# A linear-attention layer with a squared-ReLU network: r loaded for four batches at once, the diagonal added at y's eviction, the state moved to GpSimd

## The chip, the cores and the metric

One Trainium2 chip, one core. Each engine (TensorE = PE, VectorE = DVE, ScalarE = ACT, GpSimd = POOL, SyncE = SP) works through its own instructions in the order in which the program lists them. The metric is device time in microseconds: median 190.98 of three runs (190.21 to 191.86).

## What is computed

```python
# B 4, H 8, S 768, D 48; d_model = H*D = 384, d_ff 2048
for t in range(S):
    cur = einsum('bhd,bhe->bhde', u * kt, vt)
    y[:, :, t] = einsum('bhd,bhde->bhe', rt, state + cur)
    state = w[:, :, None] * state + einsum('bhd,bhe->bhde', kt, vt)
x = y.transpose(0, 2, 1, 3).reshape(B * S, H * D)
h = relu(x @ w_in)
out = (h * h) @ w_out
```

Inputs and output are float32; the kernel multiplies in bfloat16.

## The kernel before

The sequence is cut into 6 chunks of 128 tokens; a unit is one chunk of one batch, so there are 24 units, the four batches of chunk 0 first. In a unit the recurrence is a product of matrices: r scaled by powers of w (`wpos`) and k by inverse powers (`wneg`) are multiplied to a 128x128 table per head (`at`), the part above the diagonal is kept (`mask`), and the table times v, plus r times the state of the chunks before (`stb`), plus the diagonal with u, is y.

**Loads.** `load` (L190 to L197) brings r, k and v of one unit, one SP transfer each, with 128 tokens on 128 partitions; each head and token is a piece of 48 numbers, 192 bytes. Six units' loads fit at a time. The network's weights come in four quarters each, I0 to I3 for `w_in` and O0 to O3 for `w_out`, issued from POOL by `weights` (L199 to L208); a copy of one column of a k tile (`gate`) makes POOL wait for that k first.

**A unit's steps.** DVE scales r and k into one padded bf16 tile, 64 columns a head (L217). ACT casts v to `vb` (L221). The scaled tile is turned so that the head's columns lie on partitions: for the first six units (NPE) by eight PE transposes into PSUM (L236) and one ACT copy (L241), later by one transposing transfer on SP (L226). DVE multiplies turned r and k (`rk`, L246); PE makes `at` with eight products (L254), and from `rk` and u the diagonal's weight per token and head (`diag`, L268); DVE masks (L262) and multiplies that weight with v (`dv`, L276). The state's product is eight PE products of 64 by 48, one a head (L285); DVE adds it to the float32 state (L295) and multiplies by the chunk's decay (L299; L293 does the first chunk's), and ACT casts it to `stb` in two halves (L305). The last chunk has no state step. y is summed in one PSUM tile: eight products with the masked table (L313), four with the state (L319), and one that adds `dv` by way of the identity (L324). ACT evicts y (L332), it is turned again, by three PE transposes and an ACT copy in the first six units (L343, L348), by a transposing transfer afterwards (L337).

**The network.** A unit's x goes through four quarters: 12 PE products (`mm1`, L358), Relu on ACT into float32 (L366), the square on DVE into bf16 (L370), and four PE products that sum in PSUM (`mm2`, L377). ACT copies the sum out (L384), and SP stores it (L388). Three PSUM banks are shared by h and the PE transposes, two by `at` and the state's product, two by o; y has one.

**The order of the work.** It is not written by hand: the class `Plan` holds every step with its engine, a cost in microseconds, a rank, the steps that it needs and the buffers that it takes. `run` goes forward in time, and whenever an engine is free, takes of its steps that can start the one of lowest rank; the program is emitted in that order. All transfers count as one more engine, DMA, though the weights are issued from POOL. A step's rank grows by 4 a unit; `mm1` is put L1 = 10 ranks behind its unit, `mm2` L2 = 18. The front of the loads is a list: U0, U1, I0, U2, I1, U3, I2, I3, U4, O0 to O3, U5 (U is a unit's r, k and v). `room` has the buffers of each kind.

Of the kernel before, what the change touches and what calls it, by code (L numbers as in the profile page):

```python
# [79 lines left out]
def kernel(  # L80
# [11 lines left out]
    nc = tc.nc  # L92
# [10 lines left out]
    NPAD = 4  # L103

    const = ctx.enter_context(tc.tile_pool(name="const", bufs=1))
    loads = ctx.enter_context(tc.tile_pool(name="loads", bufs=6))
    work = ctx.enter_context(tc.tile_pool(name="work", bufs=4))
# [36 lines left out]
    iota_i = const.tile([128, 1], mybir.dt.int32)  # L144
    nc.gpsimd.iota(iota_i, pattern=[[0, 1]], base=0, channel_multiplier=1)
    up = const.tile([128, 1], F32)
    nc.vector.tensor_scalar(up, iota_i, 1.0, -float(C // 2), ALU.mult, ALU.add)
    down = const.tile([128, 1], F32)
    nc.vector.tensor_scalar(down, iota_i, -1.0, float(C // 2 - 1), ALU.mult, ALU.add)
    lnw = const.tile([128, dm], F32)  # L150
    nc.scalar.activation(lnw, w_bc, AF.Ln)
    wpos = const.tile([128, H, D], F32)
    nc.scalar.activation(wpos.rearrange("p h d -> p (h d)"), lnw, AF.Exp, scale=up)
    wneg = const.tile([128, H, D], F32)
    nc.scalar.activation(wneg.rearrange("p h d -> p (h d)"), lnw, AF.Exp, scale=down)

    rkw_b = [const.tile([128, 2, HP, 2, 64], BF16, name=f"rkw{n}") for n in range(NPAD)]
    for n in range(NPAD):
        for x in range(2):
            nc.vector.memset(rkw_b[n][:, x, :, :, D:], 0.0)  # L160
# [28 lines left out]

    def load(i, name):  # L190
        c, b = units[i]
        src = {"rt": r, "kt": k, "vt": v}[name]
        x = loads.tile([C, H, D], F32, name=name)
        nc.sync.dma_start(  # L194
            out=x, in_=src[b, :, c * C : (c + 1) * C, :].rearrange("h s d -> s h d")
        )
        tiles[i][name] = x  # L197
# [15 lines left out]
    def scale(i, x):  # L213
        t = tiles[i]
        t["rkw"] = rkw_b[i % NPAD]
        src, wx = (t["kt"], wneg) if x else (t["rt"], wpos)
        nc.vector.tensor_tensor(t["rkw"][:, x, :, :, :D], pair(src), pair(wx), ALU.mult)  # L217

    def cast_v(i):
        tiles[i]["vb"] = work.tile([C, H, D], BF16, name="vb")  # L220
        nc.scalar.copy(tiles[i]["vb"], tiles[i]["vt"])  # L221

    def turn_dma(i):
        t = tiles[i]
        t["rkT"] = work.tile([128, 2, HP, C], BF16, name="rkT")
        nc.sync.dma_start_transpose(  # L226
            out=t["rkT"].rearrange("p a h c -> p (a h) c"),
            in_=t["rkw"].rearrange("p a h o e -> p (a h o e)"),
        )

    def turn(i, x):
        t = tiles[i]
        if x == 0:
            t["tp"] = ps_h.tile([128, 2, HP, C], BF16, name="h")
        for p in range(HP):
            nc.tensor.transpose(t["tp"][:, x, p, :], t["rkw"][:, x, p].rearrange("p o e -> p (o e)"), identb)  # L236

    def evict_rk(i):
        t = tiles[i]
        t["rkT"] = work.tile([128, 2, HP, C], BF16, name="rkT")  # L240
        nc.scalar.copy(t["rkT"], t["tp"])  # L241

    def rk(i):
        t = tiles[i]
        t["rk"] = work.tile([128, HP, C], BF16, name="rk")
        nc.vector.tensor_tensor(t["rk"], t["rkT"][:, 0], t["rkT"][:, 1], ALU.mult)  # L246

    def at(i):
        t = tiles[i]
        t["at"] = [ps_at.tile([C, HP, C], F32, name="at") for o in range(2)]  # L250
        for p in range(HP):
            for o in range(2):
                sl = slice(o * 64, o * 64 + 64)
                nc.tensor.matmul(  # L254
                    out=t["at"][o][:, p, :], lhsT=t["rkT"][sl, 1, p, :], rhs=t["rkT"][sl, 0, p, :],
# [17 lines left out]
    def diag_v(i):  # L273
        t = tiles[i]
        t["dv"] = work.tile([C, H, D], BF16, name="dv")
# [4 lines left out]
    def state_mm(i):  # L280
        t = tiles[i]
        t["s"] = ps_at.tile([128, HP, D], F32, name="at")
        for h in range(H):
            p, o = divmod(h, 2)
            nc.tensor.matmul(  # L285
                out=t["s"][o * 64 : o * 64 + 64, p, :], lhsT=t["rkw"][:, 1, p, o, :],
                rhs=t["vb"][:, h, :], start=True, stop=True,
            )

    def state_add(i):  # L290
        c, b = units[i]
        if c == 0:
            nc.vector.tensor_tensor(st32[b], tiles[i]["s"], wend, ALU.mult)  # L293
# [234 lines left out]
```

## Time and profile before

| | |
|---|---|
| median of three runs | 190.98 us |
| the profiled execution | 190.88 us, of which the span of its instructions 189.1 |
| busy in the span | PE 169.1, DVE 145.1, ACT 112.4, POOL 11.4 us |
| transfers on SP's queue | 104832 packets, 25.37 MB, 73.4% of 16 transfer engines' span |
| weights on POOL's queue | 3712 packets, 10.5% |
| one r, k or v load | 192 KB, from issue to landing 4.1, 3.9 and 4.4 us |
| granted PE clock | 0.996 |

Busy times are of instructions as the profiler records them; those of one engine can overlap by some tens of nanoseconds, and an engine's own sums over its groups are then larger than its busy time. Matmul ends are modelled, so starts are the surer times. A row of the timeline has the start, the length, the engine, the line, the operation, the tiles written and read, and the shapes; a row of the windows the stretch, its length, the busy time of PE, PE's weight loads, DVE, ACT and POOL (with the number of instructions), then the granted clock, the share of the transfer engines and GB/s.

### The profile page before, as it was taken

To read this page: it belongs to the slowest core of one execution; us is meant where nothing else is said; L and a number is where in the kernel's file an instruction comes from. 1 tells how busy PE (TensorE), PEld (TensorE's weight loads), DVE (VectorE), ACT (ScalarE), POOL (GpSimd) and SP (SyncE) were. 2 spreads that over 40 slices of the span, in tenths; PEclk is the share of its full clock that TensorE was granted. 3 is DMA by queue.
4 is the path that set the end of the run, shared out by engine and by line. 5 is a ranking of instruction groups with operands and counts; after the bars stand their busy time and mean duration, and the time that the engine had idled before them with its cause. 6 is when DMAs were issued, how large, how long until landed. Compare 5 with 4: busy or idle time off the path is not lost.

```text
span 189.1 us, 5640 instructions
## 1 busy us (share of the span) xinstructions
PE 169.1 (89%) x2346; PEld 131.0 (69%) x2346; DVE 145.1 (77%) x292; ACT 112.4 (59%) x224; POOL 11.4 (6%) x36
## 2 busy tenths in 40 slices
PE   0269889999999998899999999979999999999991
PEld 0147779677787866677767876758777787787860
DVE  3367679967999859798989998789998888845510
ACT  3537588767756757466467557645747555555511
POOL 2261370000000000000000000000000000000000
PEclk9999999999999999999999999999999999999998
DMA  5999999918997978787989779998998999210112
GB/s 104 179 182 217 212 211 194 190 25 207 159 224 155 123 166 192 147 179 168 172 181 203 145 144 214 100 203 171 190 192 170 183 179 168 68 32 30 45 42 85
DMA packets 109545, 29.07 MB, mean 154 GB/s; under 512 B 102736, under 2 KB 109520, under 8 KB 109520
## 3 DMA queue, kind: packets, MB, share of 16 engines
q1 hardware_dynamic: 104832, 25.37, 73.4%
q0 software_dynamic: 3712, 3.15, 10.5%
q8 instruction: 18, 0.29, 0.7%
q10 hardware_dynamic: 976, 0.20, 0.7%
q14 instruction: 7, 0.06, 0.1%
HBM read 20.65 MB, written 4.72 MB: 134 GB/s over the span
## 4 chain that ended last, share of the span: by engine, by line
PE 63%; DMA 23%; DVE 5%; ACT 3%; SPq 2%; issue 2%; POOL 0%; ACTq 0%; POOLq 0%
PE o L377 27%; PE h L358 25%; DMA rkT<-rkw 8%; DMA kt<-in_k_dram 7%; DMA rt<-in_r_dram 5%; DMA w_in_sb<-in_moe_w_in_dram 4%; PE at L254 3%; DVE g L370 2%; PE y L313 2%; PE at L285 2%; SPq L194 1%; PE y L324 1%; ACT gr L366 1%; PE y L319 1%; DVE am L262 1%
## 5 line engine op out<-in xcount | busy, mean ns | idle before, releaser
L358 PE MATMUL h<-xT,w_in_sb 128*128 128x128 bf16 x1152 | 80.9, 222 | 1.7 <-DMA w_in_sb<-in_moe_w_in_dram 1.1
L366 ACT ACTIVATE gr<-h 128x512 f32<-128x512 f32 x96 | 56.7, 597 | 37.7 <-PE h L358 29.0
L358 PEld LDWEIGHTS <-w_in_sb 128*128 128x128 bf16 x1152 | 71.3, 99 | 10.6 <-DMA w_in_sb<-in_moe_w_in_dram 1.6
L377 PE MATMUL o<-w_out_sb,g 128*128 128x384 bf16 x384 | 76.6, 326 | 0.0
L370 DVE TENSOR_TENSOR g<-gr 128x512 bf16<-128x512 f32 x96 | 64.5, 686 | 12.1 <-ACT gr L366 12.0
L377 PEld LDWEIGHTS <-g 128*128 128x128 bf16 x384 | 33.3, 97 | 15.7
L262 DVE TENSOR_TENSOR am<-at,smask 128x512 bf16<-128x512 f32 x48 | 31.5, 684 | 3.3 <-PE at L254 3.1
L221 ACT CAST vb<-vt 128x384 bf16<-128x384 f32 x24 | 12.3, 511 | 16.1 <-DMA vt<-in_v_dram 15.8
L217 DVE TENSOR_TENSOR rkw<-rt,wpos 128x384 bf16<-128x384 f32 x24 | 13.3, 553 | 8.6 <-DMA rt<-in_r_dram 5.6
L217 DVE TENSOR_TENSOR rkw<-kt,wneg 128x384 bf16<-128x384 f32 x24 | 13.3, 554 | 4.3 <-DMA kt<-in_k_dram 4.3
L332 ACT CAST yb<-y 128x384 bf16<-128x384 f32 x24 | 11.5, 478 | 7.4 <-PE y L324 7.3
L305 ACT CAST stb<-st 64x192 bf16<-64x192 f32 x40 | 14.0, 349 | 2.4 <-DVE st L293 1.9
L384 ACT COPY osb<-o 128x384 f32<-128x384 f32 x24 | 11.5, 478 | 5.3 <-PE o L377 4.9
L246 DVE TENSOR_TENSOR rk<-rkT 128x512 bf16<-128x512 bf16 x24 | 10.1, 422 | 5.5 <-DMA rkT<-rkw 3.3
L236 PE MATMUL h<-identb,rkw 128*128 128x128 bf16 x48 | 6.2, 270 | 8.8 <-DVE rkw L217 8.8
L276 DVE TENSOR_TENSOR dv<-vb,y 128x384 bf16<-128x384 bf16 x24 | 13.1, 546 | 0.9 <-PE y L268 0.9
L254 PE MATMUL at<-rkT 64*128 64x128 bf16 x192 | 10.2, 229 | 1.8 <-DMA rkT<-rkw 1.8
L236 PEld LDWEIGHTS <-rkw 128*128 128x128 bf16 x48 | 3.8, 116 | 10.2 <-DVE rkw L217 9.8
L254 PEld LDWEIGHTS <-rkT 64*128 64x128 bf16 x192 | 5.8, 98 | 7.0 <-DMA rkT<-rkw 3.3
L313 PE MATMUL y<-vb,am 128*128 128x48 bf16 x192 | 9.0, 186 | 1.0 <-DVE dv L276 1.0
L313 PEld LDWEIGHTS <-am 128*128 128x128 bf16 x192 | 8.1, 98 | 2.5 <-issue 1.1
L324 PE MATMUL y<-dv,identb 128*128 128x384 bf16 x24 | 8.2, 340 | 0.0
(41 smaller groups left out, 78.0 us busy)
## 6 DMA issues: line engine op xcount, KB each, us to landing
rt<-in_r_dram SPq DMA_DIRECT2D x24, 192.0 KB, 4.1
kt<-in_k_dram SPq DMA_DIRECT2D x24, 192.0 KB, 3.9
vt<-in_v_dram SPq DMA_DIRECT2D x24, 192.0 KB, 4.4
out_dram<-osb SPq DMA_DIRECT2D x24, 192.0 KB, 3.1
w_in_sb<-in_moe_w_in_dram POOLq DMA_DIRECT2D x4, 384.0 KB, 6.6
w_out_sb<-in_moe_w_out_dram POOLq DMA_DIRECT2D x4, 384.0 KB, 10.0
rkT<-rkw SPq DMA_TRANSPOSE x18, 3.7
xT<-yb SPq DMA_TRANSPOSE x18, 3.6
```

Of the source, the lines that this page charges most:

```text
L217: nc.vector.tensor_tensor(t["rkw"][:, x, :, :, :D], pair(src), pair(wx), ALU.mult)
L221: nc.scalar.copy(tiles[i]["vb"], tiles[i]["vt"])
L254: nc.tensor.matmul(out=t["at"][o][:, p, :], lhsT=t["rkT"][sl, 1, p, :], rhs=t["rkT"][sl, 0, p, :], start=True, stop=True,)
L262: nc.vector.tensor_tensor(am, t["at"][o], smask.unsqueeze(1).to_broadcast([C, HP, C]), ALU.mult)
L276: nc.vector.tensor_tensor(t["dv"], t["vb"], t["y"][:, dm:].unsqueeze(2).to_broadcast([C, H, D]), ALU.mult)
L305: nc.scalar.copy(stb[b][sl, :, o * D : (o + 1) * D], st32[b][sl])
L313: nc.tensor.matmul(out=y[:, 2 * p + o, :], lhsT=t[f"am{o}"][:, p, :], rhs=t["vb"][:, 2 * p + o, :], start=False, stop=False, skip_group_ch ...
L332: nc.scalar.copy(t["yb"], t["y"][:, :dm])
L358: nc.tensor.matmul(out=t["h", q][:, a, :], lhsT=w_in_sb[:, n, f * 128 : (f + 1) * 128], rhs=t["xT"][:, n, :], start=(n == 0), stop=(n == N ...
L366: nc.scalar.activation(t["gr", q], t["h", q], AF.Relu)
L370: nc.vector.tensor_tensor(t["g"][:, q * 4 : q * 4 + 4, :], t["gr", q], t["gr", q], ALU.mult)
L377: nc.tensor.matmul(out=t["o"], lhsT=t["g"][:, f, :], rhs=w_out_sb[:, f, :], start=(f == 0), stop=(f == NF - 1),)
```

## The change

**r.** One tile of r now holds a chunk of all four batches: partition 32b + p has tokens 4p to 4p + 3 of batch b, so a piece of 4 x 48 numbers, 768 bytes, is read in one go. Each batch is a load of its own, into 32 partitions. DVE scales by the token's place among the four, j (`wpos` gets a power table for each j), into `rw`. The turned r comes out with its columns by j; for the first two chunks (RPE) PE turns and ACT writes the columns in their order with a step of 4, later two transposing transfers a chunk turn, and POOL puts the columns in order, one copy a unit (`order_r`). k keeps its load and has a padded tile and turn of its own, half as large.

**The diagonal.** `dv` becomes float32, and DVE adds it while it evicts y; the identity product goes.

**The state.** Four PE products a unit over pairs of heads, 128 by 96, of which two blocks are wanted; ACT copies these from PSUM, and POOL adds, decays and casts.

**Engines.** vb goes from ACT to POOL, every second square from DVE to ACT, the stores from SP to ACT. The plan's costs follow, and its list of first transfers begins R0, U0, U1, I0, with R1 ahead of U4 (R is a chunk's r, U now k and v).

```diff
-    front = ["U0", "U1", "I0", "U2", "I1", "U3", "I2", "I3", "U4", "O0", "O1", "O2", "O3", "U5"]
+    front = ["R0", "U0", "U1", "I0", "U2", "I1", "U3", "I2", "I3", "R1", "U4", "O0", "O1", "O2", "O3", "U5"]
+    def power_r(j):
+        nc.scalar.activation(wpos[:, :, j, :], lnw, AF.Exp, scale=up[:, j : j + 1])
+    def load_r(c, b):
+        if b == 0:
+            chunks[c]["r"] = rloads.tile([128, H, J * D], F32, name="r")
+        nc.sync.dma_start(
+            out=chunks[c]["r"][b * PJ : (b + 1) * PJ],
+            in_=r[b, :, c * C : (c + 1) * C, :].rearrange("h (p j) d -> p h (j d)", j=J),
+        )
+    def scale_r(c, j0, j1):
+        x = chunks[c]["rw"] = rw_b[c % 2]
+        nc.vector.tensor_tensor(
+            x[:, j0:j1].rearrange("p j a o e -> p j (a o) e")[:, :, :, :D],
+            chunks[c]["r"].rearrange("p h (j d) -> p j h d", j=J)[:, j0:j1],
+            wpos.rearrange("p h j d -> p j h d")[:, j0:j1],
+            ALU.mult,
+        )
+    def evict_r(c, j):
...
+        nc.scalar.copy(
+            t["rT"].rearrange("e b a p j -> e a b p j")[:, :, :, :, j],
+            t["tp", j // 2][:, j % 2].rearrange("e a (b p) -> e a b p", b=B),
+        )
+    def turn_r_dma(c, j):
...
+        nc.sync.dma_start_transpose(
+            out=t["rX"][:, j : j + 2].rearrange("e j a x -> e (j a) x"),
+            in_=t["rw"][:, j : j + 2].rearrange("p j a o e -> p (j a o e)"),
+        )
+    def order_r(c, b):
...
+        nc.gpsimd.tensor_copy(
+            t["rT"][:, b].rearrange("e a p j -> e a j p"),
+            t["rX"][:, :, :, b * PJ : (b + 1) * PJ].rearrange("e j a p -> e a j p"),
+        )
     def cast_v(i):
...
-        nc.scalar.copy(tiles[i]["vb"], tiles[i]["vt"])
+        nc.gpsimd.tensor_copy(tiles[i]["vb"], tiles[i]["vt"])
     def state_mm(i):
...
-        t["s"] = ps_at.tile([128, HP, D], F32, name="at")
-        for h in range(H):
-            p, o = divmod(h, 2)
+        t["s"] = ps_at.tile([128, HP, 2 * D], F32, name="at")
+        for p in range(HP):
             nc.tensor.matmul(
-                out=t["s"][o * 64 : o * 64 + 64, p, :], lhsT=t["rkw"][:, 1, p, o, :],
-                rhs=t["vb"][:, h, :], start=True, stop=True,
+                out=t["s"][:, p, :], lhsT=t["kw"][:, p].rearrange("p o e -> p (o e)"),
+                rhs=t["vb"][:, 2 * p : 2 * p + 2, :].rearrange("p h d -> p (h d)"),
+                start=True, stop=True, skip_group_check=True,
             )
+    def state_evict(i):
...
+            nc.scalar.copy(t["ssb"][sl], t["s"][sl, :, o * D : (o + 1) * D])
+    def state_next(i):
...
+        if c > 0:
+            nc.gpsimd.tensor_tensor(new, new, st32[b], ALU.add)
+        nc.gpsimd.tensor_tensor(st32[b], new, wend, ALU.mult)
     def state_cast(i):
...
-            nc.scalar.copy(stb[b][sl, :, o * D : (o + 1) * D], st32[b][sl])
+            nc.gpsimd.tensor_copy(stb[b][sl, :, o * D : (o + 1) * D], st32[b][sl])
     def y_mm(i):
...
-        nc.tensor.matmul(
-            out=t["y"][:, :dm], lhsT=identb, rhs=t["dv"].rearrange("p h d -> p (h d)"),
-            start=False, stop=True, skip_group_check=True,
-        )
     def evict_y(i):
...
-        nc.scalar.copy(t["yb"], t["y"][:, :dm])
+        nc.vector.tensor_tensor(t["yb"], t["y"][:, :dm], t["dv"].rearrange("p h d -> p (h d)"), ALU.add)
     def square(i, q):
...
+        if q % 2:
+            nc.scalar.activation(g, t["gr", q], AF.Square)
+        else:
+            nc.vector.tensor_tensor(g, t["gr", q], t["gr", q], ALU.mult)
     def store(i):
...
-        nc.sync.dma_start(out=out[b * S + c * C : b * S + (c + 1) * C, :], in_=tiles[i]["osb"])
+        nc.scalar.dma_start(out=out[b * S + c * C : b * S + (c + 1) * C, :], in_=tiles[i]["osb"])
-    room = dict(ld=6, rkw=NPAD, ..., rkT=4, ...)
+    room = dict(ld=6, r=2, rw=2, rX=2, rT=2, kw=NPAD, ..., kT=4, ..., ssb=4)
```

## The prediction

> **What bounds the kernel now.** I read the page's busy rows first, then the slices, then the chain, and last the timeline and the windows around what the change touches.
>
> ```profile
> span 189.1 us, 5640 instructions
> PE 169.1 (89%) x2346; PEld 131.0 (69%) x2346; DVE 145.1 (77%) x292; ACT 112.4 (59%) x224; POOL 11.4 (6%) x36
> PE   0269889999999998899999999979999999999991
> DVE  3367679967999859798989998789998888845510
> ACT  3537588767756757466467557645747555555511
> POOL 2261370000000000000000000000000000000000
> PE 63%; DMA 23%; DVE 5%; ACT 3%; SPq 2%; issue 2%; POOL 0%; ACTq 0%; POOLq 0%
> ```
>
> PE is full from the sixth slice to the last but one. DVE runs second at eight or nine tenths; ACT has room, and POOL does nothing after 27 us. Two thirds of the chain is PE, a quarter is transfers. The windows say where PE is not busy:
>
> ```profile
> 0.00:30.00 30.00, 18.25 (x246) 14.98 (x247) 18.02 (x48) 17.38 (x32) 11.45 (x36) 1.00 1.14 185
> 30.00:180.00 150.00, 145.94 (x2073) 113.25 (x2074) 126.38 (x244) 93.65 (x191) 0.00 (x0) 1.00 0.84 153
> 180.00:189.10 9.10, 4.93 (x31) 2.74 (x28) 0.69 (x1) 1.32 (x3) 0.00 (x0) 0.93 0.18 66
> ```
>
> After the length comes PE's busy time. So 189.1 = 169.1 busy + 11.75 idle in the front (0 to 30 us, the transfers at 1.14 of their engines) + 4.06 idle in the middle + 4.17 in the tail (last eviction and store). A microsecond of PE work removed after 30 us is a microsecond of the end, as long as no other engine needs more than PE per unit of 128 tokens. In the chain one unit takes 6.67 us (at L254 at 130.40 and 137.07), in the last chunk, which has no state product, 6.35 (150.12, 156.47).
>
> **PE.** Three edits.
>
> ```profile
> 66.04 0.81 PE L377 MATMUL o<-w_out_sb,g 128*128 128x384 bf16 x4
> 66.79 0.31 PE L285 MATMUL at<-vb,rkw 128*64 128x48 bf16 x8
> 67.03 0.84 PE L358 MATMUL h<-xT,w_in_sb 128*128 128x128 bf16 x12
> 67.71 0.36 PE L313 MATMUL y<-vb,am 128*128 128x48 bf16 x8
> 67.91 0.33 PE L319 MATMUL y<-stb,rkT 128*128 128x96 bf16 x4
> 68.08 0.33 PE L324 MATMUL y<-dv,identb 128*128 128x384 bf16 x1
> ```
>
> Ends are modelled, so I price by starts. Four 384-column products of L377 take 0.65 us in the chain, 0.162 each; the identity product of L324 has that shape, and 24 of them go: -3.9 us. The eight state products occupy PE from 66.69 (66.04 + 0.65) to 67.03, 0.34 us; the four that replace them have the shape of L319's four, 67.91 to 68.08, 0.17 us. The entry from full-array work costs 0.10 of the 0.34; were it to stay, the saving would be 0.07. I take 0.17, since the new form is L319's: 20 x 0.17 = -3.4 (bound -1.4). The transposes go from 48 to 32 for r plus 24 for k, 8 more at 0.056 (twelve L358 products of the same shape in 0.67): +0.4. PE: **-6.9 us** (bounds -4.9, -6.9).
>
> **DVE and ACT.** On DVE 48 squares (x 0.686 = 32.9), the state's add and decay (5.6 + 5.6 + 1.4) and 24 r scalings (13.3) go. The new r scalings are 8 of 384 columns (0.553) and 8 of 768 (0.95, by the step from 0.553 at 384 to 0.686 at 512), 12.0; y's eviction with the add comes, 24 x 0.546, the row of the other mixed PSUM and SBUF product, 13.1. Together 145.1 - 58.8 + 25.1 = 111. ACT gives up vb 12.3, stb 14.0, yb 11.5 and rkT 6.1, and gets 48 squares at the Relu's 0.597 (28.7), 40 state evictions at 0.349 (14.0), 14 half-size turned evictions at 0.59 (8.2; the strided writes of r may double their share, +4.7), three more exponentials (1.8) and 24 store issues at 0.42 to 0.52 (12): 112.4 - 43.9 + 64.7 = 133. Per unit ACT then needs 4 Relus 2.39, 2 squares 1.19, state 0.70, osb 0.48, store 0.5 = 5.3 us of PE's 6.33 (6.67 - 0.16 - 0.17). Behind a store issue stand the next Relus; three h buffers give PE some 4 us before it misses one. Neither engine is the bound: priced at nothing.
>
> **POOL**, which gets vb, the state and r's column order. No row shows it on a long operand. The nearest is the 128x128 select, 292 ns, against 198 for 128x4: 0.76 ns an element over 198 from below, and 292/128 = 2.28 ns an element from above. A unit's vb (384), two state operations (192 each), two casts (192 each) and one ordering copy (512) come to 2.4 to 3.8 us of 6.33. I take 2.9, nearer the row with its fixed part. Below PE, so nothing by itself; the state has four units, some 25 us, until it is used. But POOL and DVE meet:
>
> ```profile
> 8.96 0.56 DVE L217 TENSOR_TENSOR rkw<-rt,wpos 128x384 bf16<-128x384 f32 x1 [1.55 <-DMA rt<-in_r_dram]
> 9.06 0.51 POOL L181 TENSOR_TENSOR wend_c<-wend_c 128x4 f32<-128x4 f32 x1
> ```
>
> The same POOL operation takes 0.198 alone; here 0.508, ending 0.06 us after DVE's scaling. So DVE's operations on two SBUF tensors hold POOL back to their end. Whether POOL holds DVE back no row shows: nothing (DVE's 0.557 there is its usual length) up to the whole rest of a POOL operation. DVE's two-SBUF operations are then 2 squares 1.37, k 0.55, r 0.48, rk 0.42 = 2.8 us a unit. Of 4.5 such, half (2.9/6.33) would meet a POOL operation and wait half of its 0.5: 0.55 us a unit, against 1.4 that DVE is relieved of (34 over 24 units). Cost 0, or, if half of 20 x 0.55 falls on PE's path, +5.5; I take 0, since the row shows no delay of DVE, and leave the rest to a rival.
> The Trainium skill (SBUF — State Buffer, Who interferes with whom) says that a DVE instruction with two SBUF inputs and a GpSimd instruction that reads SBUF exclude each other, and whichever starts second fully blocks; the row shows the one direction, and by the rule the other would be paid too, and the sum would be some 5 us longer (an estimate).
>
> **Transfers.** r moves in 768-byte instead of 192-byte pieces: 256 packets a load instead of 1024. In the packet records the 192-byte ones took 17.4 ns (mean), so a load costs 1024 x 17.4 / 16 = 1.11 us of the engines. No plain load of 768 bytes is there: w's 1536-byte packets took 83 ns (median), so half is 41.5, 0.66 us a load; the weights' converting 768-byte ones took 78, 1.25 us. I take 0.66, the plain kind. The middle is freed of 24 x 0.45 = 11 us of 159.
> A rule speaks against it: the Trainium skill (SBUF — State Buffer, Door 1: The DMA port swizzle) gives a transfer to 32 partitions half the ports, 189 GB/s at 1 MiB against 328 for 128; from that I estimate 1.04 us a load, and the sum would be about 2 us longer. No run here shows such a load.
>
> Front, by what lies ahead of each weights gate: for I0 r0 k0 v0 r1 k1, 5 x 1.11 = 5.55, becomes four r loads and k0 v0 k1, 5.97; for I1 8.88 becomes 8.19; for I2 12.21 becomes 10.41; for O0 15.54 becomes 15.27. So +0.4, -0.7, -1.8, -0.3; at 1.25 us a load +2.8, +1.7, +0.6, +4.5. Against it stands POOL's order: vb and the first state operations, 1.5 us a unit, now share the queue with the weights.
>
> ```profile
> POOL gate L200 <- DMA kt<-in_k_dram: 8.1, 3, 3.8
> ...
> SPq L388 <- ACT osb L384: 26.6, 8, 10.4
> ```
>
> The first line (waits: total, times, longest) says that POOL's gates stood idle for kt 8.1 us in three spells, which is room for most of that; cost 0 to +2. vb of unit 0 comes after POOL's setup, at 10.95 + 0.5, and its first reader started at 12.61: hidden. Unit 0 also waits for four exponentials (4.85 + 4 x 0.61 = 7.3), four scalings, turns and evictions, about 10.5 against L254's 11.15 now; its h products wait for I0 at 17.15 anyhow. Front: **0** (-2 to +4.5).
>
> Middle: the chain's stalls there are rt, kt and rkT arriving late (66.8, 72.5, 81.8, 91.0 and 118.5 us). r comes a chunk ahead, and SP, which stood 26.6 us at stores with loads queued behind, no longer issues them. On SP's queue 24 stores of 0.52 us go (-12.5) and the transposes' issues of 1.3 us rise from 36 to 44 (+10). Of 4.06 us I take **-1.0** (-4, all of it, to +5.5, the holds).
>
> **Sum.** 189.1 - 6.9 + 0 - 1.0 = 181.2; around the span lie 190.88 - 189.1 = 1.8: **183.0 us**, 4.2% under the median of 190.98, which the profiled execution (190.88) stands beside. Its own range is 178 (front -2, middle -4) to 187.5 (front +4.5).
>
> **Rivals.** (1) The shared way of POOL and DVE decides; the end is *slower*. DVE's 2.8 and POOL's 2.4 to 3.8 us come to 5.2 to 6.6 a unit if they exclude each other, and each of POOL's six operations adds the 0.06 us seen behind DVE's end, 0.36. PE's unit is 6.33, so the point from which it decides is POOL at 3.2 us a unit. At 3.8 a unit takes 7.0, 0.65 more than PE; over the 18 or so units behind the front +12: 195 us. For it: the 0.51, and that 3.2 lies inside POOL's bounds. Against it: only DVE is seen to hold POOL, and my 2.9 lies below. Chance 0.22. (2) r's loads are not cheaper (1.25 us), so the change does not do what it says: +2.5 in the front, +1 in the middle, 186.5. For it the 78 ns, against it the 41.5. Chance 0.15. (3) ACT's and POOL's in-order queues make up for PE's saving: stores, squares and Relus in turn delay h buffers, weights come 2 us late, and the middle loses 4 more: 183 + 7 = 190. Chance 0.10. The forecast has 0.53.
>
> A measurement of this kernel tells a change from none at about 1%. Faster takes the forecast and (2), 0.68; within 1% 0.11, which is (3); slower 0.21. The range reaches from 178 to 194, most of (1) included.
>
> **What would show it.** PE busy 162; L324's group gone; the state product x80 about 0.17 us a unit. DVE near 111, ACT near 133 with store issues, POOL 60 to 90. DVE's squares and scalings still 0.55 to 0.69 if POOL doesn't hold them. r loads landing no later than k's. Wrong if DVE waits appear with POOL as releaser, if PE idles for vb, rT or stb, or if weights land after 26 us for I2.

## The result, and the profile after

The changed kernel takes 204.76 us (median; 204.38 to 205.34) where the kernel before takes 191.07 in the same comparison: 1.070 times as long, with an interval of 1.064 to 1.076. The forecast was 183.0, with a range up to 194. Its profiled execution has a span of 203.5 us against 189.1.

From the page of the changed kernel, the busy rows, five of the rows by slices (tenths of a slice of 5.1 us) and the chain by engine:

```profile
span 203.5 us, 5599 instructions
PE 167.6 (82%) x2250; PEld 132.1 (65%) x2250; DVE 133.3 (65%) x222; ACT 129.6 (64%) x235; POOL 91.3 (45%) x156
PE   0135887499999997889599997977899999999992
DVE  3235877526599994979479696888778765552210
ACT  2675496965877565575537764755677676667741
POOL 3381681903167993549626694559643100000000
PEclk9999999759999999999969999999999999999998
PE 46%; DMA 18%; DVE 18%; ACT 6%; issue 5%; POOL 3%; SPq 2%; ACTq 1%; DVEq 0%; POOLq 0%
```

Before, PE stood at 8 or 9 from the fourth slice nearly to the end, but for one 7. Now it is full only from slice nine, and has holes between slices 16 and 30; it is full again after that. DVE's share of the chain has gone from 5% to 18%, and PE's from 63% to 46%. No engine has become a bound: DVE, ACT and POOL have less to do than PE. The granted clock falls below full in slices 8, 9 and 21; behind the first three slices PE stands lowest in slices 8 and 20, at 4 and 5 tenths.

The windows of the changed kernel, with the columns as before (length; busy PE, PE's loads, DVE, ACT, POOL; clock, transfer share, GB/s), and those of the two low stretches of the clock:

```profile
0.00:30.00 30.00, 13.74 (x184) 11.47 (x185) 15.78 (x41) 17.86 (x30) 15.49 (x47) 1.00 0.97 183
30.00:180.00 150.00, 134.16 (x1855) 105.97 (x1853) 112.64 (x175) 98.88 (x184) 75.85 (x110) 0.97 0.78 148
```
```profile
38.20:45.00 6.80, 5.28 (x33) 3.72 (x33) 1.31 (x3) 5.61 (x7) 2.22 (x5) 0.50 1.26 188
103.10:106.50 3.40, 3.40 (x34) 2.72 (x32) 2.19 (x3) 1.23 (x2) 1.23 (x2) 0.50 0.90 181
```

PE is busy 4.5 us less in the first 30 us and 11.8 us less in the next 150, although it has less work to do in all. To set work and loss apart in every run, I price each product by its start-to-start time in a filled stretch (w_in 55.8 ns, w_out 162.5, the identity product 162, table 55, transposes 56, the state's products and y's with the state 42, masked table and diagonal 25) and call the rest of the span **lost**. Before, that is 162.1 of work and 27.0 lost; after, 155.2 and 48.3. So the work fell by 6.9 us, and the loss rose by some 21: 10.6 in the first 50 us, 10.5 from 50 to 150 us, nothing at the end.

Lost time is not idle time alone. In the two stretches with a granted clock of 0.50, PE got through 2.7 us of work in 5.3 busy us and through 1.85 in 3.4, so some 4 us of the loss are work done at half the clock, 2.6 in the front and 1.6 in the middle. The kernel before stands at 1.00 up to 180 us. Each of the two stretches starts in or just behind a stall of PE; no run shows whether the stall brings it on.

| kernel | time, us | span | work | lost 0 to 50 | 50 to 150 | rest | first table | first w_out product |
|---|---|---|---|---|---|---|---|---|
| before | 191.07 | 189.1 | 162.1 | 18.1 | 4.7 | 4.3 | 11.2 | 32.7 |
| after | 204.76 | 203.5 | 155.2 | 28.7 | 15.2 | 4.2 | 16.8 | 39.7 |
| e1 weights first | 200.38 | 198.6 | 155.2 | 25.5 | 13.7 | 4.1 | | 37.6 |
| e2 evict in one run | 202.44 | 200.6 | 155.2 | 25.8 | 15.4 | 4.3 | 14.2 | |
| e3 POOL only writes | 206.49 | 204.7 | 155.2 | 27.4 | 16.3 | 5.6 | | |
| e5 r early | 209.18 | 207.4 | 155.2 | 30.6 | 16.9 | 4.9 | | |
| e7 both e1 and e5 | 203.27 | 201.5 | 155.2 | 26.1 | 15.9 | 4.0 | | |
| e9 plan as measured | 193.22 | 191.4 | 155.2 | 30.4 | 1.8 | 4.0 | 15.9 | 39.5 |
| e13 delays alone | 201.79 | 199.8 | 155.2 | 26.9 | 13.9 | 4.0 | 16.9 | 40.1 |
| e17 costs alone | 198.23 | 196.1 | 155.2 | 29.1 | 7.7 | 4.0 | 15.6 | 41.3 |
| e14 and the front mended | 188.50 | 186.5 | 155.2 | 24.6 | 2.6 | 4.1 | 12.9 | 37.3 |
| e18 and r behind | 187.24 | 185.3 | 155.2 | 21.2 | 4.8 | 4.1 | 13.2 | 34.2 |
| e4 PE savings alone | 188.91 | 185.4 | 154.8 | 20.0 | 4.9 | 5.7 | 11.1 | 34.4 |
| e6 all but r's path | 198.0 | 196.2 | 154.8 | 26.2 | 9.8 | 5.5 | 11.2 | 39.6 |
| e10 e4, state on POOL | 193.37 | 191.6 | 154.8 | 25.8 | 3.9 | 7.0 | 11.1 | 37.9 |
| e11 e4, vb on POOL | 190.07 | 188.3 | 154.8 | 20.9 | 6.8 | 5.9 | 11.3 | 35.6 |
| e12 e4, stores on ACT | 190.76 | 188.7 | 154.8 | 21.2 | 8.5 | 4.2 | 11.2 | 35.6 |
| e15 before, delays | 190.62 | 188.2 | 162.1 | 21.1 | 0.2 | 4.5 | 10.2 | 36.9 |
| e16 e4, delays | 187.72 | 184.6 | 154.8 | 21.8 | 3.6 | 4.5 | 10.1 | 37.8 |

Times of after, e4, e8, e12, e14, e15, e16 and e18 are medians of several executions, the others one execution each; the kernel before stood at 190.8 to 192.3 beside them. The last five columns are of one profiled execution, whose time for e4 was 187.17.

### The profile page after: what moved, and what is told of

The parts are those of the page before. It is cut to its first block, busy times and chain, and to the rows that moved or that the text cites. A ratio compares the mean times of both kernels' runs of the same rounds, so it can differ in the third digit from the quotient of the medians.

```text
span 203.5 us, 5599 instructions
## 1 busy us (share of the span) xinstructions
PE 167.6 (82%) x2250; PEld 132.1 (65%) x2250; DVE 133.3 (65%) x222; ACT 129.6 (64%) x235; POOL 91.3 (45%) x156
## 3 DMA queue, kind: packets, MB, share of 16 engines
q1 hardware_dynamic: 82176, 20.39, 54.8%
## 4 chain that ended last, share of the span: by engine, by line
PE 46%; DMA 18%; DVE 18%; ACT 6%; issue 5%; POOL 3%; SPq 2%; ACTq 1%; DVEq 0%; POOLq 0%
PE o L456 19%; PE h L433 18%; DMA r<-in_r_dram 5%; DVE g L449 5%; ACT rT L240 4%; DVE am L337 4%; DMA w_in_sb<-in_moe_w_in_dram 3%; DMA kT<-kw 3%; DMA ucol<-in_u_dram 3%; DVE kw L293 3%; DMA kt<-in_k_dram 3%; DMA rX<-rw 2%; DVE rk L320 2%; DVE yb L407 2%; PE at L329 2%
## 5 line engine op out<-in xcount | busy, mean ns | idle before, releaser
L449 DVE TENSOR_TENSOR g<-gr 128x512 bf16<-128x512 f32 x48 | 40.3, 841 | 17.3 <-ACT gr L441 17.3
L447 ACT ACTIVATE g<-gr 128x512 bf16<-128x512 f32 x48 | 30.3, 631 | 1.5
L320 DVE TENSOR_TENSOR rk<-rT,kT 128x512 bf16<-128x512 bf16 x24 | 14.9, 623 | 22.3 <-DMA kT<-kw 8.2
L376 POOL TENSOR_TENSOR ssb<-ssb,st 128x192 f32<-128x192 f32 x16 | 10.8, 672 | 31.1 <-ACT ssb L370 31.1
L258 POOL COPY rT<-rX 128x512 bf16<-128x512 bf16 x16 | 22.4, 1498 | 3.2 <-DMA rX<-rw 2.9
L297 POOL CAST vb<-vt 128x384 bf16<-128x384 f32 x24 | 15.1, 632 | 11.6 <-DMA vt<-in_v_dram 11.1
L377 POOL TENSOR_TENSOR st<-ssb,wend_c 128x192 f32<-128x192 f32 x20 | 14.3, 716 | 12.4 <-ACT ssb L370 9.4
L370 ACT COPY ssb<-at 64x192 f32<-64x192 f32 x40 | 12.4, 311 | 11.3 <-PE at L359 10.0
L383 POOL CAST stb<-st 64x192 bf16<-64x192 f32 x40 | 18.6, 465 | 1.6
L293 DVE TENSOR_TENSOR kw<-kt,wneg 128x384 bf16<-128x384 f32 x24 | 16.1, 669 | 3.1 <-DMA kt<-in_k_dram 3.1
L407 DVE TENSOR_TENSOR yb<-y,dv 128x384 bf16<-128x384 f32 x24 | 13.2, 551 | 4.1 <-PE y L392 2.2
L232 PE MATMUL h<-identb,rw 128*128 128x128 bf16 x32 | 3.6, 272 | 13.9 <-POOL uwb L187 9.3
L351 DVE TENSOR_TENSOR dv<-vb,y 128x384 f32<-128x384 bf16 x24 | 13.1, 547 | 1.4 <-PE y L343 1.3
```

The costliest lines, as they stand in the source:

```text
L258: nc.gpsimd.tensor_copy(t["rT"][:, b].rearrange("e a p j -> e a j p"), t["rX"][:, :, :, b * PJ : (b + 1) * PJ].rearrange("e j a p -> e a j ...
L293: nc.vector.tensor_tensor(t["kw"][:, :, :, :D], pair(t["kt"]), pair(wneg), ALU.mult)
L297: nc.gpsimd.tensor_copy(tiles[i]["vb"], tiles[i]["vt"])
L320: nc.vector.tensor_tensor(t["rk"], r_of(i), t["kT"], ALU.mult)
L383: nc.gpsimd.tensor_copy(stb[b][sl, :, o * D : (o + 1) * D], st32[b][sl])
L407: nc.vector.tensor_tensor(t["yb"], t["y"][:, :dm], t["dv"].rearrange("p h d -> p (h d)"), ALU.add)
```

## The front: where the first 10 us went

PE and ACT of the changed kernel, from 9 to 17 us of the timeline (first PE, then ACT):

```profile
9.33 0.61 PE L232 MATMUL h<-identb,rw 128*128 128x128 bf16 x4 [9.33 <-POOL uwb L187]
11.33 1.01 PE L232 MATMUL h<-identb,rw 128*128 128x128 bf16 x8 [1.39 <-ACT rT L240]
14.43 0.58 PE L232 MATMUL h<-identb,rw 128*128 128x128 bf16 x4 [2.09 <-ACT rT L240]
16.82 0.40 PE L329 MATMUL at<-rT,kT 64*128 64x128 bf16 x4 [0.95 <-ACT kT L315]
...
9.98 1.30 ACT L240 COPY rT<-h 128x512 bf16<-128x512 bf16 x1 [1.12 <-PE h L232]
11.95 2.43 ACT L240 COPY rT<-h 128x512 bf16<-128x512 bf16 x2 [0.67 <-PE h L232]
15.05 1.29 ACT L240 COPY rT<-h 128x512 bf16<-128x512 bf16 x1 [0.67 <-PE h L232]
```

Turning r of the first chunk takes from 9.33 to 16.34, because each eviction takes 1.3 us, and PE and ACT take turns at it: the brackets show PE waiting for `rT` and ACT for `h`. The first table starts at 16.82, 5.7 us later than before.

POOL of the changed kernel, four rows of its timeline:

```profile
19.55 0.49 POOL L377 TENSOR_TENSOR st<-ssb,wend_c 128x192 f32<-128x192 f32 x1 [4.47 <-ACT ssb L370]
...
21.60 0.18 POOL L277 COPY gate<-kt 128x1 f32<-128x1 f32 x1
...
34.87 0.50 POOL L377 TENSOR_TENSOR st<-ssb,wend_c 128x192 f32<-128x192 f32 x1 [4.30 <-ACT ssb L370]
...
36.67 0.39 POOL L277 COPY gate<-kt 128x1 f32<-128x1 f32 x1
```

The gates are POOL copies that let a weight quarter go. They wait for nothing themselves; they stand behind a state step that POOL had already reached and that waited 4.47 and 4.30 us for ACT. The third `w_in` quarter goes at 21.6 where it went at 18.24, the first `w_out` quarter at 29.6 (23.35), the last at 39.6 (26.55).

**e1: the weights first.** The first chunk's state steps come behind all weights in the plan.

```diff
-  ("st", i), POOL, ... needs=[("ssb", i), ("stb", before) if c else None]
+  ("st", i), POOL, ... needs=[("ssb", i), ("stb", before) if c else ("O", NQ - 1)]
```

> The changed kernel, with one need more in the plan: the first chunk's state steps on POOL stand behind all eight weight transfers in POOL's order. Theory Q (the weights are late because they queue on POOL behind state operations that wait for ACT): the gate of O0 leaves before 25 us instead of 29.6, that of O3 before 31 instead of 39.6, the first product with w_out starts some 6 us earlier than 43.45, and the whole is 4 to 8 us shorter than the changed kernel's 204.8. Theory E (r's strided evictions and the four loads hold the front): weights earlier, the whole within 1.5 us.

200.38 us: the front's loss fell by 3.2 us, and the first w_out product came 2.1 earlier, at 37.6 instead of 39.7 (the 43.45 of the expectation is a later one). The gate of the last quarter went from 39.6 to 32.8. But that of the first w_out quarter, expected before 25, stayed where it was:

```profile
29.43 0.18 POOL L277 COPY gate<-kt 128x1 f32<-128x1 f32 x1 [11.31 <-DMA kt<-in_k_dram]
```

With no state step ahead of it, it waited 11.31 us for the fifth unit's k. The state steps on POOL are a cause, but not the whole; e18 takes up that k.

**e2: the turned r evicted in one run**, into contiguous columns, which leaves r's columns in the wrong order in the first two chunks.

```diff
-  t["rT"].rearrange("e b a p j -> e a b p j")[:, :, :, :, j],
+  t["rT"].rearrange("e b a p j -> e (b a p j)")[:, j * n : (j + 1) * n],
```

> The changed kernel, but the first two chunks' turned r is copied from PSUM in one run, so r's columns are left in the wrong order there. Theory E: an eviction takes 0.59 us instead of 1.32, the first table of unit 0 starts at 13 to 14 us instead of 16.8, and the whole is 2 to 5 us shorter than 204.8. Theory Q: the evictions shrink alike, the weights' gates move by less than 2 us, the whole by less than 1.5.

The eviction's group on ACT, in e2 and, further below, in e14:

```profile
L241 ACT COPY rT<-h 128x512 bf16<-128x512 bf16 x8 | 4.5, 588 | 2.9 <-PE h L232 2.9
```

588 ns against 1320 or so, the first table at 14.2, the front's loss down by 2.9 us: 202.44.

## The middle: a hold, late transfers, or the order

POOL and DVE groups of the changed kernel (after the bar: busy us, mean ns of one, then the idle time before them), and DVE's square in e3 and in e9:

```profile
L258 POOL COPY rT<-rX 128x512 bf16<-128x512 bf16 x16 | 22.4, 1498 | 3.2 <-DMA rX<-rw 2.9
L377 POOL TENSOR_TENSOR st<-ssb,wend_c 128x192 f32<-128x192 f32 x20 | 14.3, 716 | 12.4 <-ACT ssb L370 9.4 <-DVE yb L407 1.7
L449 DVE TENSOR_TENSOR g<-gr 128x512 bf16<-128x512 f32 x48 | 40.3, 841 | 17.3 <-ACT gr L441 17.3
L337 DVE TENSOR_TENSOR am<-at,smask 128x512 bf16<-128x512 f32 x48 | 30.9, 682 | 3.9 <-PE at L329 3.8
```
```profile
L450 DVE TENSOR_TENSOR g<-gr 128x512 bf16<-128x512 f32 x48 | 33.0, 688 | 20.3 <-ACT gr L442 20.2
```
```profile
L449 DVE TENSOR_TENSOR g<-gr 128x512 bf16<-128x512 f32 x48 | 37.8, 789 | 23.4 <-ACT gr L441 23.3
```

The hold that rival (1) names is there, in both directions. The square, two SBUF operands, took 686 ns before and takes 841 now; the mask, of which one operand is in PSUM, keeps its 682. POOL's decay takes 716 on average and 495 at the least.

**e3: POOL only writes.** Each long POOL operation becomes a one-column copy, for its wait, and a memset of the same output; what POOL computes is left out.

```diff
-  nc.gpsimd.tensor_copy(tiles[i]["vb"], tiles[i]["vt"])
+  nc.gpsimd.tensor_copy(gate, tiles[i]["vt"][:, 0, :1])
+  nc.gpsimd.memset(tiles[i]["vb"], 0.1)
```

> The changed kernel, but every long POOL operation (v's cast, r's order, the state's add, decay and cast) is a copy of one column, which keeps the wait, and a memset of the same output: what POOL computes is left out, and it reads next to nothing. Theory H (POOL's reads and DVE's operations on two SBUF tensors hold each other): DVE's squares fall from 0.84 to 0.69 us, rk from 0.62 to 0.43, the scaling of k from 0.67 to 0.55, PE's idle time from 60 to 150 us falls from 11 to about 5, and the whole is 6 to 10 us shorter than 204.8. Theory T (the middle loses to late transfers on SP's queue): DVE's lengths fall as well, but the middle's idle time stays above 8 and the whole within 3 us.

DVE's square is back at 688 ns, DVE's busy time fell from 133.3 to 118.6 and POOL's from 91.3 to 64.6, and the time is 206.49, no shorter. The hold is real, and taking it away doesn't shorten this kernel.

**e5 and e7: r earlier**, loads and scaling of a chunk's r put 20 ranks ahead in the plan, and POOL's ordering copies 10 ranks, each behind the one before; e7 has e1's edit too.

```diff
-  ("r", c, b), DMA, ... rank=place.get(f"R{c}", a - 24 + 0.01 * b)
+  ("r", c, b), DMA, ... rank=place.get(f"R{c}", a - 44 + 0.01 * b)
-  ("rw", c, j), DVE, ... rank=a - 8 + 0.01 * j
+  ("rw", c, j), DVE, ... rank=a - (8 if c < RPE else 28) + 0.01 * j
-  ("rT", B * c + b), POOL, ... rank=a + 4 * b - 2, needs=[...]
+  ("rT", B * c + b), POOL, ... rank=a + 4 * b - 12, needs=[..., ("rT", B * c + b - 1) if b else None]
```

> The changed kernel with other ranks for r from the third chunk on: a chunk's four loads, its scalings, its two transposing transfers and POOL's ordering copies stand about a chunk earlier in the queues of SP, DVE and POOL. Theory R (in the middle each chunk's first units wait for a chain of r load, scaling, transpose and ordering that starts too late): PE's loss from 50 to 150 us falls from 15 to about 7, the whole from 204.8 to 195 to 199. Theory H (POOL and DVE hold each other): the holds stay, the middle still loses 12 or more, the whole stays within 3 us.

> The first experiment and the earlier r together: the weights ahead of the first chunk's state on POOL, r a chunk early. If the two are separate, their gains add: about 4.4 for the weights and 6 to 10 for r, 190 to 195 us. If they share a cause, the second adds less than 3 to 200.4.

209.18 and 203.27, 4.4 and 2.9 us longer than without the earlier r; the middle's loss is 16.9 and 15.9. That r's chain is merely late falls as a theory.

What does hold PE up can be read from one of its stalls. PE of the changed kernel, and DVE in the same microseconds:

```profile
97.63 0.40 PE L329 MATMUL at<-rT,kT 64*128 64x128 bf16 x8
...
99.30 0.24 PE L343 MATMUL y<-uwb,rk 128*128 128x8 bf16 x4
101.82 0.33 PE L359 MATMUL at<-vb,kw 128*128 128x96 bf16 x4 [2.28 <-DVE am L337]
101.99 0.81 PE L456 MATMUL o<-w_out_sb,g 128*128 128x384 bf16 x4
```
```profile
100.01 0.56 DVE L293 TENSOR_TENSOR kw<-kt,wneg 128x384 bf16<-128x384 f32 x1 [2.64 <-DMA kt<-in_k_dram]
100.48 0.69 DVE L449 TENSOR_TENSOR g<-gr 128x512 bf16<-128x512 f32 x1
101.08 1.28 DVE L337 TENSOR_TENSOR am<-at,smask 128x512 bf16<-128x512 f32 x2
102.28 0.55 DVE L351 TENSOR_TENSOR dv<-vb,y 128x384 f32<-128x384 bf16 x1
```

PE's state product waits 2.28 us for the mask. The table that the mask reads was made from 97.63 on, in 0.40 us; DVE could have masked from about 98.0 on. But the order lists a later unit's scaling `kw` ahead of it, and that waited 2.64 us for its k to land. In the plan a step is ready when its cost and its delay (`lag`) have passed, so k was down as there 1.07 + 2.0 = 3.1 us after its issue and r 0.55 + 2.0 = 2.6; the profile has 4.1 and 5.2. It also had POOL's ordering copy at 0.75 us (1.50 in the profile) and the strided eviction at 0.5 (1.32). An instruction that the plan thinks ready is put in an in-order queue, and when it isn't, all behind it waits.

**e9: the plan as measured.** No instruction is changed; the planner's figures are set to the profile's or near them, and with them the order in which the same instructions are listed. (With cost and delay k is now down for 4.6 us and r for 4.75, near the 4.1 and 5.2; the turn of k for 4.2, above its 2.6. The 2 us of the expectation are the delay alone.) The list of the figures is in part:

```diff
-  (name, i), DMA, 1.07, do(load, i, name), ... lag=2.0,
+  (name, i), DMA, 1.07, do(load, i, name), ... lag=3.5,
-  ("rT", B * c + b), POOL, 0.75, do(order_r, c, b),
+  ("rT", B * c + b), POOL, 1.5, do(order_r, c, b),
-  ("kT", i), DMA, 0.85, do(turn_dma, i), ... lag=2.0,
+  ("kT", i), DMA, 1.2, do(turn_dma, i), ... lag=3.0,
```

> The changed kernel with nothing of its work altered; only the planner's costs and delays are set to what the profile after shows (a transfer lands 3 to 5 us after issue where it had 2, the ordering copy 1.5 us where it had 0.75, the strided eviction 1.2 where it had 0.5, and so on), so that the order in which each engine lists its instructions changes. Theory L: the middle's extra PE loss of some 10 us comes from an order planned with too early transfers, which puts instructions that wait at the head of DVE's and ACT's in-order queues; then the loss from 50 to 150 us falls from 15 to about 8 and the time to 195 to 198. Theory C (the transfers' own later landing and the longer operations are the cause, in whatever order): the loss in the middle stays at 13 to 17, the time at 201 to 207.

193.22 us. The stretch from 50 to 150 us, in the windows of the changed kernel and of e9:

```profile
50.00:150.00 100.00, 88.80 (x1239) 69.77 (x1238) 81.21 (x123) 63.81 (x124) 64.18 (x89) 0.98 0.91 172
```
```profile
50.00:150.00 100.00, 99.36 (x1447) 79.11 (x1445) 88.70 (x140) 73.11 (x143) 70.25 (x96) 1.00 0.95 175
```

And the waits of that stretch (total, times, longest), of DVE and of PE, in the changed kernel and then in e9:

```profile
DVE rk L320 <- DMA kT<-kw: 7.6, 6, 1.9
...
DVE kw L293 <- DMA kt<-in_k_dram: 2.9, 2, 2.6
DVE rw L220 <- DMA r<-in_r_dram: 2.4, 3, 0.9
...
PE at L359 <- DVE am L337: 8.2, 8, 2.3
PE y L392 <- DVE dv L351: 1.7, 2, 1.1
```
```profile
DVE rk L320 <- DMA kT<-kw: 2.0, 3, 1.4
...
PE y L392 <- DVE dv L351: 0.4, 1, 0.4
```

DVE's waits for transfers fall from 12.9 us to 2.0, PE's waits for the mask and `dv` behind them from 9.9 to 0.4, and PE is at 99.36 of 100 us. The lost time of the middle is 1.8 us, with the hold still there (the square at 789 ns). The middle's loss was the order of the list. It is one execution, but not one lucky list: e14 and e18 below, two more lists from the same figures, lose 2.6 and 4.8 there. In e9 the front is no better (30.4), and the time is still not under that of the kernel before.

**e13 and e17: delays alone, costs alone.** The two halves of e9's figures.

```diff
 e13: lag=2.0 -> 3.0 to 5.0 on the transfers, the costs left
 e17: costs of w, r, rw, rTj, rT, scale, vb, kT, rk, xT, sq as in e9, lag=2.0 left
```

> The changed kernel with the planner's transfer delays alone set to what the profile shows (r 4.0, k and v 3.5, the transposing ones 3.0 to 3.5, weights 5.0 us, all 2.0 before); costs of operations stay. If late transfers at the head of in-order queues are the middle's cause (theory L in its narrow form): the loss from 50 to 150 us at 2 to 5, time 192 to 197. If the operations' costs (POOL's copies 1.5 for 0.75, DVE's and ACT's by some tenths) are what the order lacked: middle 12 to 16, time 201 to 206.

> The changed kernel with the planner's operation and transfer costs as measured, the delays left at 2.0 us. If the costs are what the order lacked: loss from 50 to 150 us 1 to 4, time 192 to 196. If costs and delays are needed together: middle 8 to 15, time 198 to 205.

Middle 13.9 and 7.7. The narrow form of the theory, that only the transfers' delays were wrong, falls: the delays alone change little there (DVE still waits 13.7 us for transfers in that stretch), the costs take half, and only both take all.

## What each part of the change costs

**e4: the three PE savings alone**, on the kernel before: the identity product goes and DVE adds `dv` at y's eviction, the state's product by head pairs (DVE adds the two halves from PSUM), every second square on ACT. r, vb, the state's arithmetic and the stores stay as before.

```diff
-  nc.tensor.matmul(out=t["y"][:, :dm], lhsT=identb, rhs=t["dv"]..., ...)
-  nc.scalar.copy(t["yb"], t["y"][:, :dm])
+  nc.vector.tensor_tensor(t["yb"], t["y"][:, :dm], t["dv"]..., ALU.add)
-  ("sq", i, q), DVE, 0.64,
+  ("sq", i, q), ACT if q % 2 else DVE, 0.53 if q % 2 else 0.64,
```

> The kernel before, with only what lightens PE: the diagonal added by DVE at y's eviction, the state's product over head pairs with DVE adding its two halves from PSUM, and every second square on ACT. r's loads, v's cast, the state and the stores stay as they were, POOL has the weights alone. If the prediction's price of PE is right (7.3 us: 24 x 0.162 and 20 x 0.17) and nothing else is late, 182 to 185 us. If DVE, which gets the eviction and a second half add, or ACT in the squares' place turn late, 186 to 191.

188.91 us against 192.28 beside it, 0.987 times (0.978 to 0.996). The work fell by 7.3 us, the loss rose by 3.6.

**e8**, the same with the second squares of the first five units left on DVE:

```diff
-  if q % 2:
+  if q % 2 and i >= 5:
```

> The fourth experiment (PE's savings alone), with the squares of the first five units left on DVE, since in its front ACT's copies of turned r and k stood before the squares. If ACT was what its front lost 1.9 us by, 185 to 186.5 us where that kernel's profiled execution took 187.2; if not, 187 to 189.

190.34 us, 0.9905 (0.9846 to 0.9964), with 6.5 us lost in the middle: no better than e4, and outside both of its expected ranges.

**e6: all but r's path**, so e4 with vb and the state on POOL and the stores on ACT.

```diff
-  nc.scalar.copy(tiles[i]["vb"], tiles[i]["vt"])
+  nc.gpsimd.tensor_copy(tiles[i]["vb"], tiles[i]["vt"])
-  nc.vector.tensor_tensor(st32[b], st32[b], wend, ALU.mult)
+  nc.gpsimd.tensor_tensor(st32[b], new, wend, ALU.mult)
-  nc.sync.dma_start(out=out[...], in_=tiles[i]["osb"])
+  nc.scalar.dma_start(out=out[...], in_=tiles[i]["osb"])
```

> Everything of the change but r's path: r is loaded, scaled and turned with k in each unit as before, and POOL has v's cast and the state, without the ordering copy. Theory R: the middle loses about 5 us as before, the first table of unit 0 starts near 11 us, and the whole is 186 to 191; what the weights lose on POOL's queue stays. Theory H: squares and rk are still lengthened by POOL's casts and state, the middle loses 8 or more, and the whole is 192 to 197.

198.0: 10.8 over e4's profiled execution, 6.8 under the whole change, with 26.2 lost in the front and 9.8 in the middle. That is above both expected ranges; so r's path is not all, and the rest lies in the three moves of that diff. **e10, e11 and e12** make these moves one at a time.

> The three PE savings alone (187.2 us in their profiled run) with the state's add, decay and casts moved to POOL behind an eviction by ACT. Theory Q (POOL's in-order queue, shared with the weights' issues, makes the front late): first w_out product 4 to 6 us later than that kernel's 34.4, the loss from 0 to 50 us 24 to 26 instead of 20.0, the time 192 to 196. If the state on POOL is harmless and the other two moves make the 10.8 us: 186 to 189.

> The three PE savings alone with v's cast moved from ACT to POOL. Theory Q: each cast is issued between the weights' gates but waits only for its own v load, so little: first w_out product at most 1.5 us later than 34.4, time 186 to 190. If the cast by itself blocks the weights: 191 or more.

> The three PE savings alone with the 24 stores issued by ACT instead of SP. Theory Q leaves the front as it is (20 us lost, first w_out product at 34 to 35). If stores on ACT delay the Relus behind them: the loss from 50 to 150 us rises from 4.9 to 8 or more, time 190 to 193. If they free SP for the loads at no cost to ACT: 184 to 187, and this is the best kernel.

By spans the three cost 6.2, 2.9 and 3.3 us, together 12.4, near the 10.8 of e6. But e4's profiled execution is the fastest of its four: against its median of 188.91 they cost 4.5, 1.2 and 1.9 us, together 7.5, and e6 9.1. The state's is mostly front (25.8 lost there; the first w_out quarter goes at 31.4 where e4 has 22.8), as theory Q says. vb's single time of 190.07 lies inside the spread of e4's executions (187.17 to 190.3), so it can't be told from nothing. e12 is 1.003 times the kernel before (0.998 to 1.008): the stores on ACT took back what the PE savings gave, mostly in the middle, where 8.5 us are lost. That Relus wait behind the stores was expected, but the waits of that stretch show something else: DVE waits 8.8 us for k and r, against 3.6 in e4, and PE 2.2 us for the mask, against 0.2. Why these loads are later is open. All three ran with the planner's old delays.

**e14 and e18: the change with its front mended.** On e9's plan, e1's edit and an eviction of two places of j at a time, four of 1024 columns for eight of 512, with `rT` laid out to fit; in e18 the second chunk's r stands behind the fifth unit's k.

```diff
 e14, the eviction:
-  t["rT"].rearrange("e b a p j -> e a b p j")[:, :, :, :, j],
-  t["tp", j // 2][:, j % 2].rearrange("e a (b p) -> e a b p", b=B),
+  t["rT"].rearrange("e a b p j -> e (a b p) j")[:, :, j : j + 2],
+  t["tp", j // 2].rearrange("e j a x -> e (a x) j"),
 e18:
-  "I3", "R1", "U4", "O0", "O1", "O2", "O3", "U5"]
+  "I3", "U4", "O0", "O1", "R1", "O2", "O3", "U5"]
```

> The changed kernel with the measured plan, the first chunk's state on POOL planned behind all weights, and the turned r evicted by two tokens' places at a time (four evictions of 1024 columns in runs of two, for eight of 512 in single strided columns). Same computation as the change. If these two are the front's cause: the loss from 0 to 50 us falls from 30.4 to 22 to 25, first w_out product from 39.5 to 35 or so, time 184 to 188. If something else holds the front: 190 to 194.

> The version with measured plan, weights ahead of the state and paired evictions, and the second chunk's r listed behind the fifth unit's k and v instead of ahead of them. If that r is what holds the first w_out quarter: its gate falls from 29.8 to 24 to 26, first w_out product from 37.3 to 34 to 35, front loss from 24.6 to 21 to 23, time 184.5 to 187. If the fifth unit's k is late by the weights' own transfers: gate still past 28, time 187.5 to 190.

The eviction and the first `w_out` gate in e14, then that gate in e18:

```profile
L240 ACT COPY rT<-h 128x1024 bf16<-128x1024 bf16 x4 | 4.0, 1011 | 1.9 <-PE h L232 1.9
...
29.83 0.18 POOL L277 COPY gate<-kt 128x1 f32<-128x1 f32 x1 [10.55 <-DMA kt<-in_k_dram]
```
```profile
19.62 0.18 POOL L277 COPY gate<-kt 128x1 f32<-128x1 f32 x1 [0.99 <-DMA kt<-in_k_dram]
```

e14: 188.5 us, 0.983 (0.975 to 0.991). The front's loss went from 30.4 to 24.6, by the two causes named. What then held the first w_out quarter was a gate that waited 10.55 us for the fifth unit's k, issued behind four r loads. e18 puts it ahead, and the gate runs at 19.62: the front's loss is 21.2, though 2.2 us come back in the middle, and the time is 187.24 (186.56 to 187.77), 0.984 (0.977 to 0.991).

**e15 and e16: the measured delays without the change**, in the kernel before and in e4.

```diff
-  (name, i), DMA, 1.1, do(load, i, name), ... lag=2.0,
+  (name, i), DMA, 1.1, do(load, i, name), ... lag=3.5,
```

> The kernel before with the planner's delays of the transfers as measured (k, v and r loads 3.5, transposes 3.0, weights 5.0), nothing else. Its loss from 50 to 150 us is 4.7 and can't fall by more: 187 to 192. If a measured plan makes the order better wherever it is: 187 to 188.5. If the delays matter only where r must be on time for four units at once: 190 to 192.

> The three PE savings alone with the same delays. Middle loss 4.9 can fall to 2: 184 to 186 if the measured plan helps wherever it is; 187 to 189 if not. Beats the measured-plan version of the change only if that stays over 186.

The kernel before gains nothing: 190.62, 0.998 (0.994 to 1.002). Its middle goes from 4.7 lost to 0.2, and its front gives 3.0 back with a w_out product that starts 4.2 us later. e16 is 187.72, 0.982 (0.975 to 0.990). So e4, e14, e16 and e18 all beat the kernel before by 1.3 to 1.8%, and their intervals don't tell them apart: moving r and loading POOL is worth nothing over the PE savings that these runs could tell. Neither the kernel before nor e4 was run with measured costs and delays together.

## Why the prediction was wrong

**PE's work was right**: -6.9 by the sum, 162.1 to 155.2 by the count of products at the same prices; what is measured anew is that the state product and its follower start 0.17 us apart (101.82, 101.99), as taken. PE's busy time is 167.6 us and not the 162 forecast, and some 4 us of that are the two stretches at half the clock.

**"Front: 0 (-2 to +4.5)" failed**, by three of its steps: +10.6. The strided evictions were taken at 0.59 with the remark that strides may double their share; they took 1.32, and I counted four in a row where PE and ACT alternate over one tile, so "about 10.5" for the first table was 16.8. The shared queue of POOL was priced at "0 to +2" from the 8.1 us in which its gates stood idle. That counted how long POOL's new operations run, not how long they wait: a state step waited 4.5 us for ACT with the gates behind it, and the last quarter went 13 us late, of which e1 took back 6.7. And the count of loads ahead of each gate took the gate of O0 as no later; e1 and e14 show it waiting 11 us for the fifth k, and e18 that the four r loads ahead of that k cost the front 3.4. Two signs of being wrong came: PE stood idle for `rT`, and the third `w_in` quarter, issued at 21.7, landed after 26, since none of these quarters took less than 5.8 us.

**"Middle: -1.0 (-4 to +5.5)" failed**: +10.5. The freed transfers were real: SP's queue, without the stores, fell to 54.8% of the engines' span; with the 7.8% of the queue that now has the stores that is 127 us against 139, so some 11 us as computed. What the step left out is that the program's order is computed from costs and delays, and that the change put in new ones. I took the order as given and asked only whether the resources suffice. They did; in e9 PE reaches 99.36 of 100 us.

**The hold** was taken at 0, and that was right for the wrong reason. "The row shows no delay of DVE" didn't generalise: DVE was held too, its square from 686 to 841 ns, as the Trainium skill has it (SBUF — State Buffer, Who interferes with whom). But the 5 us that the rule would add don't show at the end: without the hold the kernel is no shorter (e3), and with it e9 loses 1.8 us in the middle. **Rival (1)** so had the right sign by luck, with a wrong mechanism: POOL, at 0.63 for vb, 0.67 and 0.72 for the state, 2 x 0.47 for the casts and 1.50 for the order, needs 4.45 us a unit, over the 3.2 from which it was to decide, and it didn't. **Rival (2)** is out: r's packets took 49.4 ns on average, 256 x 49.4 / 16 = 0.79 us a load, between my 0.66 and 1.25, though a load landed 5.2 us after its issue, later than k's 4.1 and against the sign that was named; the estimate from the Trainium skill (SBUF — State Buffer, Door 1: The DMA port swizzle) was 1.04, and the measurement decides. **Rival (3)**, in-order queues, is the nearest: its mechanism decided, in POOL's and DVE's queues, more than ACT's, and its "2 us late" for the weights measured 1 to 13 by their gates and its "4 more" for the middle 10.5. (The chances of (1) and (3) stand as 0.22 and 0.10 with the rivals and as 0.21 and 0.11 behind them.)

DVE at 133.3 instead of 111 and POOL at 91.3 instead of 60 to 90 set no bound: in e9 they are busy 88.70 and 70.25 of the 100 us in which PE is busy 99.36. ACT at 129.6 was near its 133.

## What to carry to other kernels

Where a planner orders the work by costs and delays, a change has two effects: what it does to the work and what it does to the order. Set the plan's figures from a profile of the changed kernel before judging the change; here that alone was worth 11 us, with not one instruction altered. In the kernel before, measured delays without the costs gave nothing (e15). When an engine's queue also issues something that others wait for, ask of each instruction put ahead of it not how long it runs but how long it may wait.

## What the runs showed of the hardware

An ACT copy from PSUM that writes single bf16 elements at a step of four took 1.32 us for 512 columns, against 0.588 into contiguous columns; in runs of two elements 1024 columns took 1.01, the time of the contiguous 1024-column copy of the kernel before (1.013). The same reordering on POOL, SBUF to SBUF, took 1.33 to 1.89 us. POOL and DVE lengthened each other (the square 686 to 841 ns, `rk` 422 to 623; POOL's decay from 495 to 716), and operations of DVE with one operand in PSUM kept their lengths (the mask 684 and 682 ns). At a granted clock of 0.50 PE did about half as much: 1.85 us of work in 3.4.
